# Attention and two expert layers on one core: TensorE's order written per unit, with the product with v one unit behind and 1/sum spread by two transposes

## The chip, the core and the metric

The kernel runs on one core of a Trainium2 chip. The metric is the device time of one execution, in microseconds (us); before the change the median of three runs is 1271.57 us (1271.40 to 1272.42). The engines are named as the profile names them: PE is TensorE (PEld its weight loads), DVE is VectorE, ACT is ScalarE, POOL is GpSimd, SP is SyncE, which only issues transfers here.

## What is computed

Attention with pooled queries, then a dense expert layer, then a second one. Inputs are float32, sizes are those of `setup`: 4 batches, 8 heads, 1152 positions, head width 64; d_model 512.

```python
q_pool = q.reshape(B, H, S // 2, 2, D).mean(axis=3)          # 576 queries a head
scores = scale * np.matmul(q_pool, k.transpose(0, 1, 3, 2))
scores = scores - np.max(scores, axis=-1, keepdims=True)
attn = np.exp(scores)
attn = attn / (np.sum(attn, axis=-1, keepdims=True) + 1e-09)
x = np.matmul(attn, v)                                       # -> (4 * 576, 512)

h = x @ w_in                                                 # 512 -> 2048
g = np.where(h >= 1, h, np.where(h <= -1, 0.0, (h + 1) ** 2 / 4))
x = g @ w_out                                                # 2048 -> 512

h = np.maximum(np.maximum(x @ w1, x @ w2), x @ w3)           # 512 -> 768
return h @ w_out2                                            # 768 -> 512
```

## The kernel before

**Units.** The attention is cut into 48 units: 4 batches b, in each 3 query blocks i of 192 pooled queries (`NB`), in each 4 pairs of heads p. Unit n is 12b + 4i + p; "unit 14" below is b = 1, i = 0, p = 2. A unit has 2 x 192 rows of scores against 1152 positions of k. They are worked on in three groups of 128 rows: group 0 and group 1 are the first 128 queries of the one head and of the other, group 2 is the rest, 64 rows of each. s0, s1 and s2 stand for the scores of the three groups (`qk`, L347: six matmuls, twelve for s2).

**One group.** `soft` makes the scores in PSUM, takes the row maximum on DVE (L361), the bias on ACT (L362) and the Exp on ACT (L363), which leaves float32 probabilities `pf` in SBUF and adds up their sum in `sm`. `turned` brings the probabilities into the transposed form `pt` that the product with v needs, and this goes two ways:

- In batches 1 to 3, groups 0 and 1 are split into a float16 high and low part `hl` (ACT L413, a subtraction on DVE L414) and transposed by a DMA, `pt<-hl` (L415), on SP's queue. Group 2 is transposed on TensorE, nine 128x128 pieces in float32 (L395), and split on the way out of PSUM (ACT L400, DVE L401).
- In batch 0 (`WHOLE`) all three groups are transposed on TensorE in float32 and copied out whole (L406, L408).

**1/sum.** `shares` forms 1/(sum + 1e-9) in `sm`, three columns of 128 rows, and spreads it into a tile of 128 x 192 that stands like the product with v: one row for each of the 2 x 64 columns of v, one column for each query. It does so by four float32 products with the identity (L376, L377), into the rest of the PSUM buffer that holds the nine transposed pieces. ACT copies it out as `R` (L379).

**The product with v.** `av` runs 54 matmuls in float16 (L432; 18 in float32 in batch 0, L427), and DVE multiplies the result by `R` (L445) into `xf`. After four units of a block `xh`, its float16 split, is ready for the dense layer.

**The dense layer** of a block is 8 tiles of up-projection (`ph`, L498, 24 matmuls each, followed by the gate on ACT, DVE and POOL, L503 to L509) and 4 of down-projection (`py`, L524, 48 matmuls each). `dense` hands them out in the turn up, up, down, in which each down belongs to the block before. The down-projections left over run after the last unit.

**Buffers in PSUM.** Scores and transposed tiles share two buffers of three banks (`place`, tag `sc`): they are given out in turn, so each `place` waits until the buffer of the one before last is read out. The product with v and the dense tiles share two banks (`psg`).

**The order.** TensorE runs in the order in which the program is written (`manual_schedule` for PE); the other engines are ordered by a scheduler that works from this text. The loop over slots, three for each unit, writes it: scores of the slot, in slot 0 the product with v of the unit two back, then `turned` of the slot before. `step` puts dense tiles in between, by a count of what is due (4 tiles for 3 slots, from slot 12 + `LAG` on). So from unit 8 on a unit has this row on TensorE: s0, product with v, a down, transposes of the unit before and 1/sum, s1, an up, s2, an up. The tables `K0`, `V0`, `K1`, `V1` name the slots in which the k and v of a batch are loaded, scaled and transposed; for batches 1 to 3 this is done in the last units of the batch before (L261 is the square that their scale comes from). The weights of the dense layer are converted during units 0 to 5, by `wgen` steps, `WR` a slot.

**After the last unit** the remaining downs run while the weights of the second layer are converted (from L150) into SBUF that the attention has given back; then the second layer, `p` (L737) and `po` (L754), takes the rest of the time.

Of the kernel before, what the change touches and what calls it, by code (L numbers as in the profile page):

```python
# [7 lines left out]
F32 = mybir.dt.float32  # L8
# [16 lines left out]
K1 = (-2, 0, 2)  # L25
V1 = (1, 3, 4)
WR = 1.5
OW = 130
OD0, T0 = -150, 48
LAG = 10  # L30
AVW = 0
POOL_KV = False
# [14 lines left out]
def body(ctx: ExitStack, tc: tile.TileContext, q, k, v, w_in, w_out, w1, w2, w3, w_o2, out):  # L47
# [320 lines left out]

    def shares(b, i, p, rs):

        sm = sums.pop((b, i, p))
        nc.vector.tensor_scalar(out=sm, in0=sm, scalar1=1e-9 * 2.0 ** 12, scalar2=None, op0=ALU.add)
        nc.vector.reciprocal(out=sm, in_=sm)
# [10 lines left out]
    def turned(b, i, p, who, pf):  # L384
# [4 lines left out]
        if who == 2 or WHOLE(b, p):  # L389

            tr = place(f"tr{key}")
            rs = tr[:, KT * P:KT * P + NB]
            tr = tr[:, :KT * P]
            for c in range(KT):
                nc.tensor.transpose(tr[:, c * P:(c + 1) * P], pf[:, c * P:(c + 1) * P], ident)  # L395
            copy = shares(b, i, p, rs) if who == 2 else None
            if not WHOLE(b, p):
                tr = tr.rearrange("p (c h q) -> p h c q", c=KT, h=2)
                hi, lo = pt[:, :, 0:KT, P:NB], pt[:, :, KT:2 * KT, P:NB]
                nc.scalar.activation(out=hi, in_=tr, func=AF.Copy)  # L400
                nc.vector.tensor_tensor(out=lo, in0=tr, in1=hi, op=ALU.subtract)  # L401
                copy()
                return
# [3 lines left out]
            else:  # L407
                nc.scalar.activation(out=pt[:, :, :, P:NB], in_=tr.rearrange("p (c h q) -> p h c q", c=KT, h=2),  # L408
                                     func=AF.Copy)
                copy()  # L410
            return
# [162 lines left out]
    def now(t):  # L574
        for gen in events.get(t, ()):
            next(gen)
# [5 lines left out]
    behind, todo = {}, []  # L582
    due = sent = wdue = 0.0
    slots = [(b, i, p, who) for b, i, p in units for who in range(3)]

    def step(t, share):

        nonlocal sent
# [5 lines left out]
    for t, (b, i, p, who) in enumerate(slots):  # L594
        n = t // 3
        if who == 0:
            exp_scale(b, i, p)
        behind[t] = soft(b, i, p, who)
        now(t)
        step(t, 0)  # L600
        if who == AVW and n >= 2:
            av(*todo.pop(0))
            step(t, .4)
        if t:
            turned(*behind.pop(t - 1))
        step(t, .8)
        if who == 2:
            todo.append((b, i, p))
        if who == 1 and n % 2 == 1 and n + 1 < len(units):
            q_prep(*units[n + 1])  # L610
        wdue += WR
        while wdue >= 1:
            with shift(OW):
                next(wgen, None)
            wdue -= 1
        step(t, 1.3)
    turned(*behind.pop(t))
    while todo:
        av(*todo.pop(0))
    order.__exit__(None, None, None)  # L620
# [217 lines left out]
```

## Time and profile before

| | |
|---|---|
| median of three runs | 1271.57 us |
| the profiled execution, its own time | 1269.06 us |
| its span, first to last instruction | 1267.2 us |
| PE busy | 1099.9 us, 87% |
| PEld busy | 892.9 us, 70% |
| DVE busy | 846.7 us, 67% |
| ACT busy | 687.3 us, 54% |
| POOL busy | 309.0 us, 24% |

The shares are means over the whole span. Units 0 to 13, the units in the middle of a batch, the units that also prepare the next batch, the rest after the last unit, and the second layer differ in what they hold, so each has its own shares. The start of a unit is read off the first matmul of its s0.

### The profile page before, as it was taken

What the parts mean: (1) busy time and instruction counts of PE and PEld (TensorE: products, weight loads), DVE (VectorE), ACT (ScalarE), POOL (GpSimd) and SP (SyncE); (2) the same over time, 40 slices, a digit from 0 to 9 for tenths busy, and PEclk for the clock granted to TensorE, in tenths of its full rate; (3) what the DMA queues carried; (4) which work ended last, traced back from release to release, by engine and by line L of the source; (5) the groups of instructions that cost most, each with busy time, mean ns of one, the idle gap of its engine ahead of it and who ended that gap; (6) DMA issues with size and microseconds to landing.
All of it is one profiled execution on the core that took longest, in us unless ns stands there. A gap on an engine that the chain in (4) does not pass through costs nothing. (4 is left out here: it accounts for less than half of the span.)

```text
span 1267.2 us, 27173 instructions
## 1 busy us (share of the span) xinstructions
PE 1099.9 (87%) x11346; PEld 892.9 (70%) x11346; DVE 846.7 (67%) x1406; ACT 687.3 (54%) x1193; POOL 309.0 (24%) x306
## 2 busy tenths in 40 slices
PE   0557799989999879899988999998968999999998
PEld 0334577767788768777776787787968877767774
DVE  4997776687777778777778977676997662232220
ACT  4777786666666666666656666665453421112111
POOL 1210113342223324222233422222654020000000
PEclk9989899999999899999988999999979999999999
DMA  9863313476555778555568655545422310000001
GB/s 314 247 179 123 92 27 72 113 155 119 107 107 99 135 164 175 101 103 104 102 146 177 123 95 95 95 82 136 160 100 83 117 52 31 9 18 26 18 17 42
DMA packets 273756, 134.94 MB, mean 106 GB/s; under 512 B 229089, under 2 KB 256737, under 8 KB 272609
## 3 DMA queue, kind: packets, MB, share of 16 engines
q1 hardware_dynamic: 273632, 133.20, 45.7%
q8 instruction: 89, 1.46, 0.5%
q14 instruction: 35, 0.28, 0.1%
HBM read 62.39 MB, written 9.44 MB: 57 GB/s over the span
## 5 line engine op out<-in xcount | busy, mean ns | idle before, releaser
L347 PE MATMUL sc<-kst,qst 128*64 128x512 f16 (+3 forms) x1152 | 179.1, 347 | 107.2 <-ACT pf L363 52.6
L361 DVE TENSOR_REDUCE st<-sc 128x1 f32<-128x1152 f32 x144 | 195.0, 1354 | 88.5 <-PE sc L347 88.4
L498 PE MATMUL ph<-xh,win 128*128 128x192 f16 x2304 | 219.8, 256 | 1.1 <-ACT t L503 0.6
L524 PE MATMUL py<-g,wou 128*128 128x192 f16 x2304 | 201.5, 247 | 15.0 <-POOL g L507 7.5
L737 PE MATMUL p<-yh,wm 128*128 128x288 f16 x1728 | 214.5, 286 | 0.0
L498 PEld LDWEIGHTS <-win 128*128 128x128 f16 x2304 | 203.0, 103 | 13.5 <-issue 8.3
L524 PEld LDWEIGHTS <-wou 128*128 128x128 f16 x2304 | 189.7, 98 | 22.6 <-issue 17.2
L347 PEld LDWEIGHTS <-qst 128*64 128x64 f16 (+1 forms) x1152 | 84.8, 108 | 170.5 <-issue 96.1
L737 PEld LDWEIGHTS <-wm 128*128 128x128 f16 x1728 | 169.0, 98 | 45.0 <-issue 0.4
L363 ACT ACTIVATE pf<-sc,st,esc 128x1152 f32<-128x1152 f32 x144 | 188.4, 1308 | 4.0
L505 POOL TENSOR_TENSOR rl<-t,rl 128x384 f32<-128x384 f32 x96 | 111.1, 1158 | 247.7 <-DVE rl L504 226.4
L362 ACT ACTIVATE st<-st,esc 128x1 f32<-128x1 f32 x144 | 42.1, 293 | 129.6 <-DVE st L361 129.2
L414 DVE TENSOR_TENSOR hl<-pf,hl 128x1152 f16<-128x1152 f32 x72 | 98.8, 1372 | 20.4 <-ACT hl L413 20.4
L395 PE MATMUL tr<-ident,pf 128*128 128x128 f32 x648 | 90.5, 288 | 20.8 <-ACT R L379 10.7
L507 POOL TENSOR_SCALAR g<-t,dgs 128x384 f16<-128x384 f32 x96 | 72.4, 754 | 134.2 <-DVE t L506 102.4
L395 PEld LDWEIGHTS tr<-ident,pf 128*128 128x128 f32 x648 | 76.1, 149 | 30.7 <-ACT R L379 14.4
L742 DVE TENSOR_TENSOR mx<-p,mx 128x288 f32<-128x288 f32 x48 | 21.9, 456 | 106.2 <-PE p L737 105.6
L745 ACT ACTIVATE h<-mx 128x288 f16<-128x288 f32 x48 | 21.2, 442 | 131.3 <-DVE mx L743 131.3
L432 PE MATMUL av<-pt,vhl 128*64 128x192 f16 x1944 | 87.1, 247 | 1.2 <-DMA pt<-hl 1.2
L432 PEld LDWEIGHTS <-vhl 128*64 128x64 f16 x1944 | 79.5, 110 | 10.3 <-issue 10.0
L413 ACT ACTIVATE hl<-pf 128x1152 f16<-128x1152 f32 x72 | 83.8, 1163 | 1.1
L509 DVE SCALAR_TENSOR_TENSOR g<-t,dgs,g 128x384 f16<-128x384 f32 x96 | 75.2, 783 | 12.1 <-POOL g L507 12.0
(167 smaller groups left out, 1338.4 us busy)
## 6 DMA issues: line engine op xcount, KB each, us to landing
kn<-in_k_dram SPq DMA_DIRECT2D x16, 576.0 KB, 4.6
vn<-in_v_dram SPq DMA_DIRECT2D x16, 576.0 KB, 4.4
raw_m<-in_moe_w_dram SPq DMA_DIRECT2D x12, 768.0 KB, 4.5
raw_in<-in_moe_w_in_dram SPq DMA_DIRECT2D x8, 1024.0 KB, 6.8
qn<-in_q_dram SPq DMA_DIRECT2D x24, 256.0 KB, 3.3
raw_ou<-in_moe_w_out_dram SPq DMA_DIRECT2D x10, 512.0 KB, 4.4
qst<-qst SPq DMA_DIRECT2D x48, 96.0 KB, 2.3
y_d<-ys SPq DMA_DIRECT2D x48, 96.0 KB, 2.0
```

The costliest lines, as they stand in the source:

```text
L347: nc.tensor.matmul(sc[m0:m1, n0:n1], qst[b, i, p][who][:, var, m0:m1], ks[:, h, n0:n1], start=(var == 0), stop=(var == 1))
L361: nc.vector.tensor_reduce(out=m, in_=sc, axis=AX.X, op=ALU.max, negate=True)
L363: nc.scalar.activation(out=pf, in_=sc, func=AF.Exp, bias=nb, scale=e, accum_out=sums[b, i, p][:, who:who + 1])
L395: nc.tensor.transpose(tr[:, c * P:(c + 1) * P], pf[:, c * P:(c + 1) * P], ident)
L413: nc.scalar.activation(out=hl[:, 0], in_=pf, func=AF.Copy)
L414: nc.vector.tensor_tensor(out=hl[:, 1], in0=pf, in1=hl[:, 0], op=ALU.subtract)
L432: nc.tensor.matmul(acc[64 * h:64 * h + 64], vhl[b, p][:, vi, h, c, :], pt[:, h, pi * KT + c, :], start=(c == 0 and e == 0), stop=(c == KT ...
L498: nc.tensor.matmul(ph[:, a], win[:, wi, kt, ff * P:(ff + 1) * P], x[:, xi, kt], start=(kt == 0 and e == 0), stop=(kt == KD - 1 and e == 2))
L505: nc.gpsimd.tensor_tensor(out=rl, in0=t2, in1=rl, op=ALU.add)
L509: nc.vector.scalar_tensor_tensor(out=g[:, 1, fs, :], in0=t2, scalar=gs, in1=g[:, 0, fs, :], op0=ALU.mult, op1=ALU.subtract)
L524: nc.tensor.matmul(py, wou[:, ff // 2, wi, ff % 2, m * P:(m + 1) * P], g[:, gi, ff, :], start=(ff == 0 and e == 0), stop=(ff == NF - 1 and ...
L737: nc.tensor.matmul(ph[:, :NB2], wm[:, wi, i, kt, ff * P:(ff + 1) * P], yh[:, yi, kt, n0:n0 + NB2], start=(kt == 0 and e == 0), stop=(kt == ...
```

## The change

TensorE's order is no longer counted out by `step` but written as a row of words for each unit, one row for batch 0 (`True`) and one for the others. "s" is a group's scores, "t" its `turned` ("t-" group 2 of the unit before), "r" `shares` of the unit before, "a1" the product with v of the unit one back, "d" the next dense tile, "q" the preparation of queries, "w" a step of the weights. Dense tiles begin with unit 6 (`DENSE`). `V1` prepares v one slot earlier in two of its steps. `shares` widens 1/sum on DVE to a tile `rb` of 128 x 192, transposes that in two pieces, and copies it out in two.

```diff
-V1 = (1, 3, 4)
+V1 = (1, 2, 3)
...
-LAG = 10
-AVW = 0
+ORDER = {True: "s0 t- d d r s1 t0 q s2 t1 a1 w d d w w",
+         False: "s0 t- d d r s1 t0 a1 s2 t1 q w d d w w"}
+DEPTH = 1
+DENSE = 6
...
-        for h in range(2):
-            rows = slice(64 * h, 64 * h + 64)
-            nc.tensor.matmul(rs[rows, 0:P], sm[:, h:h + 1].to_broadcast([P, 64]), ident, start=True, stop=True)
-            nc.tensor.matmul(rs[rows, P:NB], sm[:, 2:3].to_broadcast([P, 64]), ident[:, rows], start=True, stop=True)
-        R[b, i, p] = tp.tile([P, NB], F32, tag="R", bufs=3, name=f"R{b}_{i}_{p}")
-        return lambda: nc.scalar.activation(out=R[b, i, p], in_=rs, func=AF.Copy)
+        nc.vector.tensor_copy(out=rb, in_=sm.rearrange("p (a o) -> p a o", o=1).to_broadcast([P, 3, 64]))
+        r, half = R[b, i, p], slice(64, P)
+        nc.tensor.transpose(rs[:, 0:P], rb[:, 0:2].rearrange("p a o -> p (a o)"), ident)
+        nc.tensor.transpose(rs[:, P:2 * P], rb[:, 2, 0:1].to_broadcast([P, P]), ident)
+
+        nc.scalar.activation(out=r, in_=rs[:, :NB], func=AF.Copy)
+        nc.scalar.activation(out=r[half, P:NB], in_=rs[half, NB:2 * P], func=AF.Copy)
...
-            copy = shares(b, i, p, rs) if who == 2 else None
+            if who == 2:
+                R[b, i, p] = rs
...
-        d = (t - 12 - LAG) * 4 / 3 + share
-        while sent + 1 <= d:
-            next(dense, None)
-            sent += 1
...
-        if who == AVW and n >= 2:
-            av(*todo.pop(0))
-            step(t, .4)
...
+        elif kind == "r":
+            if n:
+                shares(*units[n - 1])
+        elif kind == "a":
+            if n >= int(num):
+                av(*units[n - int(num)])
+        elif kind == "d":
+            if n >= DENSE:
+                next(dense, None)
...
+    for n, (b, i, p) in enumerate(units):
+        for word in ORDER[WHOLE(b, p)].split():
+            attend(n, word)
```

The dense tiles still come in the turn up, up, down. A down takes two calls of `dense`, so the four "d" of a unit are two ups and one down: both ups stand ahead of "r", the down at the end.

What this moves is shown at three places of batch 2, in which unit 28 is block 1, pair 0. In the names the digits are block, pair and, for scores and transposed tiles, group (`tr_1_0_2` holds the transposes of group 2 of unit 28); the last number only tells buffers apart.

The first place is on PE, where unit 28's product with v starts. Before the change it follows s0 of unit 30 (`sc_1_2_0`):

```order
L347 LDWEIGHTS qst_1_2_6865
L347 MATMUL sc_1_2_0_6959<-kst_2_5086,qst_1_2_6865 128x512
L347 LDWEIGHTS qst_1_2_6865
L347 MATMUL sc_1_2_0_6959<-kst_2_5086,qst_1_2_6865 128x128
L432 LDWEIGHTS vhl_0_4806
L432 MATMUL av_1_0_6972<-pt_1_0_6591,vhl_0_4806 64x192
```

After it the product follows s1 of unit 29 (`sc_1_1_1`):

```order
L352 LDWEIGHTS qst_1_0_6633
L352 MATMUL sc_1_1_1_7049<-kst_1_5067,qst_1_0_6633 128x512
L352 LDWEIGHTS qst_1_0_6633
L352 MATMUL sc_1_1_1_7049<-kst_1_5067,qst_1_0_6633 128x128
L440 LDWEIGHTS vhl_0_4967
L440 MATMUL av_1_0_7066<-pt_1_0_6804,vhl_0_4967 64x192
```

The product with v has moved ahead by two groups of scores, the down-projection and one up, and it now stands between s1 and s2.

The second place is on PE too, where unit 28's 1/sum is spread, in unit 29. Before the change, between the last matmul of a down (`py`) and s1:

```order
L524 MATMUL py_1_1_6762<-g_1_5263,wou 128x192
L395 MATMUL tr_1_0_2_6815<-ident,pf_1_0_2_6643 128x128 x9
L376 MATMUL tr_1_0_2_6815<-ident,sm_1_0_6444 64x128
L377 MATMUL tr_1_0_2_6815<-ident,sm_1_0_6444 64x64
L376 MATMUL tr_1_0_2_6815<-ident,sm_1_0_6444 64x128
L377 MATMUL tr_1_0_2_6815<-ident,sm_1_0_6444 64x64
L347 LDWEIGHTS qst_1_0_6341
L347 MATMUL sc_1_1_1_6835<-kst_1_4810,qst_1_0_6341 128x512
```

After it, between the last matmul of the second up (`ph`) and s1:

```order
L506 LDWEIGHTS win
L506 MATMUL ph_2_7_7007<-xh_2_5804,win 128x192
L384 MATMUL tr_1_0_2_6962<-ident,rb_1_0_7042 128x128
L385 MATMUL tr_1_0_2_6962<-ident,rb_1_0_7042 128x128
L352 LDWEIGHTS qst_1_0_6633
L352 MATMUL sc_1_1_1_7049<-kst_1_5067,qst_1_0_6633 128x512
```

Two transposes stand in the place of four products, and the nine transposes of the same buffer have moved away from them, ahead of the two ups.

The third place is ACT, from the copy of unit 28's transposed tile (`pt_1_0<-tr_1_0_2`) in unit 29 on. Before the change:

```order
L400 ACTIVATE pt_1_0_6591<-tr_1_0_2_6815 128x2x9x64
L362 ACTIVATE st_1_1_1_6842<-st_1_1_1_6842,esc_1_1_6684 128x1
L363 ACTIVATE pf_1_1_1_6843,sm_1_1_6694<-sc_1_1_1_6835,st_1_1_1_6842,esc_1_1_6684 128x1152
L503 ACTIVATE t_1_2_4_6894<-ph_2_4_6869,hh_4156 128x384
L379 ACTIVATE R_1_0_6831<-tr_1_0_2_6815 128x192
L413 ACTIVATE hl_1_1_1_6920<-pf_1_1_1_6843 128x1152
L362 ACTIVATE st_1_1_2_6915<-st_1_1_2_6915,esc_1_1_6684 128x1
L363 ACTIVATE pf_1_1_2_6916,sm_1_1_6694<-sc_1_1_2_6902,st_1_1_2_6915,esc_1_1_6684 128x1152
```

After it:

```order
L410 ACTIVATE pt_1_0_6804<-tr_1_0_2_6962 128x2x9x64
L367 ACTIVATE st_1_1_0_6956<-st_1_1_0_6956,esc_1_1_6947 128x1
L368 ACTIVATE pf_1_1_0_6958,sm_1_1_6957<-sc_1_1_0_6949,st_1_1_0_6956,esc_1_1_6947 128x1152
L511 ACTIVATE t_1_2_6_6999<-ph_2_6_6974,hh_4001 128x384
L421 ACTIVATE hl_1_1_0_7062<-pf_1_1_0_6958 128x1152
L511 ACTIVATE t_1_2_7_7032<-ph_2_7_7007,hh_4001 128x384
L387 ACTIVATE R_1_0_7040<-tr_1_0_2_6962 128x192
L388 ACTIVATE R_1_0_7040<-tr_1_0_2_6962 64x64
L367 ACTIVATE st_1_1_1_7056<-st_1_1_1_7056,esc_1_1_6947 128x1
L368 ACTIVATE pf_1_1_1_7057,sm_1_1_6957<-sc_1_1_1_7049,st_1_1_1_7056,esc_1_1_6947 128x1152
```

The copy of 1/sum has become two (L387, L388), and they have moved from behind the Exp of s1 to ahead of it. The buffers move with the order: s2 (`sc_1_1_2`) was given the buffer of s1 before, and after the change that of the transposed tile, which the copies of 1/sum read last.

## Rows read from the trace of the kernel before

**Rows 1.** Windows by stage: start:end, length, busy (instructions) per engine, PEclk, DMA, GB/s.

```profile
148.86:163.03 14.17, 10.49 (x96) 7.50 (x96) 10.81 (x18) 11.47 (x18) 1.25 (x2) 1.00 0.07 15
163.03:177.55 14.52, 14.14 (x144) 11.27 (x144) 10.73 (x17) 13.91 (x22) 1.59 (x3) 1.00 0.20 42
...
206.82:284.61 77.79, 67.86 (x649) 56.02 (x648) 56.74 (x107) 47.76 (x83) 29.51 (x28) 0.91 0.59 130
284.61:399.45 114.84, 106.22 (x1339) 91.69 (x1338) 85.22 (x127) 75.47 (x136) 31.95 (x36) 1.00 0.57 107
399.45:516.24 116.79, 100.12 (x1166) 85.67 (x1164) 94.81 (x157) 73.05 (x130) 40.68 (x41) 0.93 0.72 148
...
614.67:710.60 95.93, 83.36 (x973) 71.61 (x972) 81.14 (x137) 61.40 (x111) 37.56 (x35) 0.93 0.72 150
...
858.25:979.97 121.72, 103.19 (x1235) 97.99 (x1233) 100.26 (x147) 55.20 (x88) 58.05 (x42) 0.93 0.42 123
```

**Rows 2.** Timeline, PE, one unit: start, busy, line, tiles, count [idle before <-releaser].

```profile
776.22 1.14 PE L347 MATMUL sc<-kst,qst 128*128 128x512 f16 x6
777.29 2.42 PE L432 MATMUL av<-pt,vhl 128*64 128x192 f16 x54
779.64 4.13 PE L524 MATMUL py<-g,wou 128*128 128x192 f16 x48
783.61 1.15 PE L395 MATMUL tr<-ident,pf 128*128 128x128 f32 x9
784.69 0.45 PE L376 MATMUL tr<-ident,sm 128*64 128x128 f32 x4
...
785.18 1.15 PE L347 MATMUL sc<-kst,qst 128*128 128x512 f16 x6
786.16 2.14 PE L498 MATMUL ph<-xh,win 128*128 128x192 f16 x24
789.54 1.17 PE L347 MATMUL sc<-kst,qst 128*64 128x512 f16 x12 [1.23 <-ACT pf L363]
790.64 2.15 PE L498 MATMUL ph<-xh,win 128*128 128x192 f16 x24
792.63 1.14 PE L347 MATMUL sc<-kst,qst 128*128 128x512 f16 x6
```

**Rows 3.** Timeline, DVE, the same unit.

```profile
786.37 1.36 DVE L361 TENSOR_REDUCE st<-sc 128x1 f32<-128x1152 f32 x1 [2.73 <-PE sc L347]
...
796.16 0.42 DVE L445 SCALAR_TENSOR_TENSOR xf<-av,Uv,R 128x192 f32<-128x192 f32 x1
```

**Rows 4.** Timeline, ACT, the same unit.

```profile
785.30 1.13 ACT L400 ACTIVATE pt<-tr 128x1152 f16<-128x1152 f32 x1 [0.67 <-PE tr L377]
...
788.09 1.31 ACT L363 ACTIVATE pf<-sc,st,esc 128x1152 f32<-128x1152 f32 x1
...
789.85 0.33 ACT L379 ACTIVATE R<-tr 128x192 f32<-128x192 f32 x1
```

**Rows 5.** DMA view of the transposing transfers of L415.

```profile
DMA to landing us min/median/max: 4.5/4.6/10.0
```

**Rows 6.** Windows, a unit that prepares the next batch.

```profile
479.60:496.90 17.30, 15.37 (x197) 13.29 (x194) 17.27 (x36) 10.71 (x21) 8.91 (x8) 1.00 0.84 175
```

**Rows 7.** Timeline, PE, another such unit.

```profile
454.49 2.00 PE L347 MATMUL sc<-kst,qst 128*64 128x512 f16 x12 [4.06 <-ACT R L379]
```

**Rows 8.** Timeline, PE, in the first batch.

```profile
144.82 1.17 PE L347 MATMUL sc<-kst,qst 128*64 128x512 f16 x12 [1.22 <-ACT pt L406]
146.44 1.20 PE L395 MATMUL tr<-ident,pf 128*128 128x128 f32 x9 [0.45 <-ACT pf L363]
...
216.53 2.18 PE L395 MATMUL tr<-ident,pf 128*128 128x128 f32 x9 [2.03 <-ACT R L379]
```

**Rows 9.** Timeline, ACT, after the last unit: the weights of the second layer.

```profile
885.51 2.59 ACT L150 ACTIVATE st_m<-raw_m 128x768 f32<-128x768 f32 x3 [4.93 <-DMA pt<-hl]
```

**Rows 10.** Timeline, DVE, after the last unit: the scaled operand of the second layer.

```profile
972.14 4.78 DVE L710 SCALAR_TENSOR_TENSOR yh<-yf,ysc,yh 128x576 f16<-128x576 f32 x4 [0.65 <-POOL yh L708]
```

More of the change, by code (lines that the diff above doesn't have):

```diff
@@ L367, in body, with shares @@
     R = {}
-    def shares(b, i, p, rs):
+    def shares(b, i, p):
         sm = sums.pop((b, i, p))
+        rs = R[b, i, p]
+        R[b, i, p] = tp.tile([P, NB], F32, tag="R", bufs=3, name=f"R{b}_{i}_{p}")
         nc.vector.tensor_scalar(out=sm, in0=sm, scalar1=1e-9 * 2.0 ** 12, scalar2=None, op0=ALU.add)
+        rb = tp.tile([P, 3, 64], F32, tag="rb", bufs=2, name=f"rb{b}_{i}_{p}")
         nc.vector.reciprocal(out=sm, in_=sm)
-        for h in range(2):
-            rows = slice(64 * h, 64 * h + 64)
-            nc.tensor.matmul(rs[rows, 0:P], sm[:, h:h + 1].to_broadcast([P, 64]), ident, start=True, stop=True)
-            nc.tensor.matmul(rs[rows, P:NB], sm[:, 2:3].to_broadcast([P, 64]), ident[:, rows], start=True, stop=True)
-        R[b, i, p] = tp.tile([P, NB], F32, tag="R", bufs=3, name=f"R{b}_{i}_{p}")
-        return lambda: nc.scalar.activation(out=R[b, i, p], in_=rs, func=AF.Copy)
+        nc.vector.tensor_copy(out=rb, in_=sm.rearrange("p (a o) -> p a o", o=1).to_broadcast([P, 3, 64]))
[4 more added lines that the diff above has]
+        nc.scalar.activation(out=r[half, P:NB], in_=rs[half, NB:2 * P], func=AF.Copy)
     def whole(pt):
@@ L391, in turned @@
             tr = place(f"tr{key}")
-            rs = tr[:, KT * P:KT * P + NB]
+            rs = tr[:, KT * P:KT * P + 2 * P]
             tr = tr[:, :KT * P]
@@ L401, in turned @@
                 nc.vector.tensor_tensor(out=lo, in0=tr, in1=hi, op=ALU.subtract)
-                copy()
                 return
@@ L409, in turned @@
                                      func=AF.Copy)
-                copy()
             return
@@ L582, in body @@
     behind, todo = {}, []
[L583 to L588, printed above, removed]
-        d = (t - 12 - LAG) * 4 / 3 + share
-        while sent + 1 <= d:
-            next(dense, None)
-            sent += 1
[L594 to L600, printed above, removed]
-        if who == AVW and n >= 2:
-            av(*todo.pop(0))
-            step(t, .4)
[L604 to L616, printed above, removed]
@@ L617, in body, with attend @@
-    turned(*behind.pop(t))
-    while todo:
-        av(*todo.pop(0))
+    wdue = 0.0
+    def attend(n, word):
+        nonlocal wdue
+        b, i, p = units[n]
+        kind, num = word[0], word[1:]
+        if kind == "s":
+            who = int(num)
+            if who == 0:
+                exp_scale(b, i, p)
+            behind[n, who] = soft(b, i, p, who)
+            now(3 * n + who)
+        elif kind == "t":
+            key = (n - 1, 2) if num == "-" else (n, int(num))
+            if key in behind:
+                turned(*behind.pop(key))
+        elif kind == "r":
[7 more added lines that the diff above has]
+                next(dense, None)
+        elif kind == "q":
+            if n % 2 == 1 and n + 1 < len(units):
+                q_prep(*units[n + 1])
+        elif kind == "w":
+            wdue += WR
+            while wdue >= 1:
+                with shift(OW):
+                    next(wgen, None)
+                wdue -= 1
@@ L620, in body @@
+    for n, (b, i, p) in enumerate(units):
+        for word in ORDER[WHOLE(b, p)].split():
+            attend(n, word)
+    last = len(units)
+    turned(*behind.pop((last - 1, 2)))
+    shares(*units[last - 1])
+    for n in range(last - DEPTH, last):
+        av(*units[n])
     order.__exit__(None, None, None)
```

## The prediction

> **What bounds the kernel now.** I read the stages first, as windows cut at the starts of units [rows 1]. From 858 us on the program is another matter (its tail is below, its last part is TensorE at full pace), so the change is worth something before that, in 48 units of attention. In the stretch from 284.61 to 399.45 seven units take 114.84 us, 16.41 each, and TensorE is busy 106.22: it waits 8.62, which is 1.23 a unit, though it is the engine that is fullest.
>
> The timeline of TensorE in one such unit shows where [rows 2]: from 776.22 to 792.63 its pieces follow each other without a break, but for one wait of 1.23 us ahead of the scores of the row rest (s2). The releaser is the Exp of the scores just before (s1): s2 was given the PSUM buffer of s1, and only one up-projection tile stands between them. The reader should see the chain behind s1 in the two engine timelines: the maximum takes 1.36 us on DVE [rows 3], the bias and the Exp end at 789.40 on ACT [rows 4], and s2 starts at 789.54; from s1's end at about 786.2 that is 3.3 us, and the cover is 2.1. A wait that nothing else of TensorE's fills, and that every unit of a stage repeats in which TensorE is the fullest engine, is worth its whole length.
>
> **The change, part by part.** All sums are against the profiled execution, 1269.06 us; the median of the runs shown is 2.5 us above it, which I add at the end.
>
> *Steady units (numbers 14 to 20, 27 to 32, 38 to 46: 22 of them).* From starts to next starts in rows 2: s0 1.07, product with v 2.35, down 3.97, nine transposes 1.08, spreading 1/sum 0.49, s1 0.98, s2 1.10, a tile of up 1.98 (790.64 to 792.63). The new order has s0, transposes, up, up, spread, s1, product with v, s2, down. Spreading becomes two transposes; at 1.08 for nine they are 0.24 together, so 0.25 is saved. The sum is 1.07 + 1.08 + 3.96 + 0.24 + 0.98 + 2.35 + 1.10 + 3.97 = 14.75, if nothing waits. What is late next is checked one by one, with 3.3 us as the price of a reduction and Exp. Exp of s0 ahead of s1: cover 5.28 (transposes, two ups, spread) against 3.3 plus 1.13 for the copy of the transposed tile on ACT [rows 4]: 0.8 to spare. Exp of s1 ahead of the next s0: cover 7.4; the reduction now stands behind a subtraction (L414) of as many elements as its own 1.36 [rows 3] and two short gate operations on DVE, so about 5.6: free. Exp of s2 ahead of its transposes: cover 5.04 (down and s0), chain 3.3 plus about 0.9 of queued DVE work: 0.8 to spare, the tightest. The evictions of 1/sum ahead of s2 (they share its buffer): two of at most 0.33 each [rows 4], done about 1.3 us after the spread, cover 3.3. So I take 14.8: 22 x 1.6 = -35. The ends are 14.75 (-37) and 15.5, with both spare times of 0.8 eaten by a DVE that runs late (-20).
>
> The new copy that widens 1/sum on DVE has no row. It is 128x192 float32, so it lies near the 0.42 of the other 128x192 operation [rows 3]; between 0 and 0.6. DVE is busy 85.22 of 114.84 us there [rows 1], 12.2 a unit; with the copy 12.6 of 14.8, so it has room. The new second eviction adds under 0.33 to an ACT that is busy 75.47 of 114.84.
>
> The product with v one unit behind adds a wait: it needs the transposing transfers of its own unit's s1, which had a unit more. Laid out in the new unit, the subtraction of s1 ends about 15 us after the unit's start; the transfer lands 4.6 us after its issue [rows 5], at 19.7; the product starts at 14.8 + 7.3 = 22.1. It is hidden with 2.4 us to spare. Behind it on TensorE stand s2 and down.
>
> *Units that also prepare the next batch's k and v (21 to 26, 33 to 37: 11 units, 116.79 + 95.93 = 212.7 us in rows 1).* Here TensorE waits up to 4.06 us for the eviction of 1/sum [rows 7], which stands in ACT's queue behind the square of a new k tile (L261), and the granted clock of both stretches is 0.93 against 1.00 in the steady one [rows 1]. After the change that eviction has 3.3 us of cover instead of 2.1, and s1 has 5.3. What remains is DVE: busy 94.81 + 81.14 = 176 us, 16.0 a unit, 16.4 with the copy. That DVE can run that full shows in the unit at 479.60, with 17.27 of 17.30 [rows 6]. I take 17.7: 11 x 17.7 = 194.7, -18. The ends are 16.4 (-32) and only the spread saved (-3).
>
> *The first batch (units 0 to 13), whose products are whole float32.* Two things count against the change. The dense work starts 1.33 units earlier, so two ups (3.96) and two downs (7.94) move in here: +11.9. And with both ups ahead of s1, only one transposed tile stands between s1 and s2, so s2 waits for its copy, 1.22 us, and the next transposes for an Exp, 0.45; a unit without dense work shows both waits [rows 8]. Units 7 to 9 wait 0.4 each (14.52 - 14.14 in the first, rows 1), so six units lose 1.3 each: +8. Against that: the spread 14 x 0.25 = -3.5, waits in units 6 and 10 to 13 (14.17 - 10.49 and 77.79 - 67.86, 13.6 us in all, rows 1; one of 2.03 in rows 8), of which the moved work fills about half, -6.5, and in units 0 to 5, where weights are converted, s1 loses the product with v as cover, +2. Sum +12; ends +5 and +25.
>
> *The tail (858.25 to 979.97, from unit 47's start to the second block, rows 1).* 11.9 us of dense work have left it, but TensorE is not alone in it: the second block's weights can only be converted when the attention's buffers are free, which ACT begins at 885.51, 27.3 us after the unit's start, behind the last transposing transfer [rows 9]. The chain from there runs through ACT, DVE and GpSimd to the scaled operand of the second block, whose first quarter is written 1.2 us after 972.14 [rows 10], 88 us on; the second block starts at 979.97 only because TensorE has downs left until then. The subtraction of unit 47 comes some 2 us sooner in the new unit, so the chain would end at 25 + 88 = 113 instead of 121.7: -9. TensorE's own work alone would give 11.9 and the unit's 1.2 (16.0 to 14.8): -13, the lower end; the upper is 0, with a later chain.
>
> Sum: -35 - 18 + 12 - 9 = -50; 1269.06 - 50 = 1219, plus 2.5: **1221 us**.
>
> **One rule against it.** The nine transposes take 1.08 us where the granted clock is 1.00 [rows 1, 2], 0.12 each. The Trainium skill says otherwise in "TensorE: Matmul & The Clock Gate", Part 4 (PE-mode transpose): a transpose costs some 275 ns in a kernel, and transposes do not raise the clock. By that figure two would be 0.55, dearer than the 0.49 they replace, and the estimate would be 1236; the trace disagrees in the steady units.
>
> **The rivals.** (a) Transposes at the lower clock level. After a wait nine took 2.18 [rows 8], 0.24 each; two would cost 0.48, what they replace: 48 x 0.25 = +12, 1233 us. Against it: they stand behind two ups without a break. The rule above belongs here. (b) DVE and the weight chain keep their pace: the units with preparation give 3 instead of 18 and the tail nothing, 1221 + 15 + 9 = 1245. For it: both stretches have DVE at 0.8 and more of the time [rows 1]; against: the wait in them is one for ACT. (c) **Slower**: the transfers land late, and the product with v waits for them in each unit of batches 1 to 3. From the layout above a unit then takes 15.05 + landing - 7.33; it loses to 16.41 from a landing of 8.7 us on. The median is 4.6, the longest 10.0 [rows 5]; at 10.0 it is 17.7, 36 x 1.3 = +47, and the first batch's +12: about 1330. Against it: the long ones are few. (d) The new order does not do what it says: s2 is again given a buffer that the Exp of s1 frees. The cover would be the product with v alone, 2.35 against 2.1 now; only 0.25 and the spread's 0.25 are won in each steady unit, the first batch costs 12, and the whole comes out at 1271.57 - 11 + 12 = 1272, the same. The built program speaks against it: s2 there waits for the eviction of 1/sum. (e) DVE fills up in the units with preparation and TensorE ends the tail: 1221 - 14 - 4 = 1203.
>
> **How the numbers follow.** Forecast 0.64, (a) 0.08, (b) 0.15, (e) 0.05, (c) 0.05, (d) 0.03. The range goes from 1203, case (e), to 1246, just past (b); it leaves out (c) and (d), half of (e) and some of the spread about (b). About 0.2%, 2.5 us, is what this kernel's measurement can tell from no change. Faster 0.92, same 0.03, slower 0.05.
>
> **What would show it.** Right: unit starts 14.8 us apart with no wait in the steady stretches, the wait of the scores for Exp gone there, two transposes of 0.12 for 1/sum, the second block starting some 50 us earlier, at about 930. Wrong: a wait of the product with v for its transfer (c), of s2 for Exp (d), periods of 19 and more with preparation (b), a granted clock below 1.00 in steady units (a), or a first batch longer by much more than 12 us.

## The result and the profile after

The changed kernel takes 1240.3 us in the median of four runs (1239.76 to 1242.11), against 1271.49 before: 0.976 of it, 95% interval 0.9743 to 0.9777. The forecast was 1221, with a range of 1203 to 1246. The sign and the range hold; of the 50 us that were forecast 31 came. The profiled execution has a span of 1237.9 us, 29.3 less than before.

The stages of the changed kernel, as windows cut at the starts of units (columns as in [rows 1]): units 0 to 5, 6 to 13, 14 to 20, 21 to 26, 27 to 32, 33 to 37, 38 to 46, and from unit 47 to the second layer.

```profile
27.53:164.50 136.97, 83.36 (x517) 56.58 (x518) 109.76 (x192) 98.74 (x154) 20.94 (x15) 0.78 0.55 159
164.50:312.93 148.43, 130.71 (x1287) 107.92 (x1286) 99.17 (x184) 96.28 (x164) 46.76 (x49) 0.94 0.39 78
312.93:421.45 108.52, 102.68 (x1297) 89.82 (x1296) 92.29 (x138) 76.62 (x144) 31.65 (x39) 1.00 0.65 115
421.45:526.78 105.33, 92.89 (x1129) 81.05 (x1127) 92.45 (x165) 74.51 (x137) 42.07 (x39) 0.98 0.82 164
526.78:618.58 91.80, 87.69 (x1113) 77.01 (x1111) 77.07 (x113) 63.81 (x121) 25.86 (x32) 1.00 0.62 111
618.58:706.61 88.03, 78.09 (x944) 68.06 (x942) 76.73 (x141) 61.65 (x114) 37.48 (x34) 0.98 0.83 162
706.61:840.28 133.67, 130.90 (x1668) 115.52 (x1666) 113.16 (x166) 96.96 (x179) 32.73 (x42) 1.00 0.58 101
840.28:948.08 107.80, 86.94 (x1023) 82.55 (x1021) 89.95 (x136) 54.75 (x91) 44.63 (x33) 0.94 0.44 130
```

Set beside the same stages of before (most of them in [rows 1]; the others by the same unit starts):

| stage | before, us | after, us | change | forecast |
|---|---|---|---|---|
| units 0 to 5 | 121.7 | 137.0 | +15.3 | about +0.5 |
| units 6 to 13 | 135.8 | 148.4 | +12.7 | about +11.5 |
| steady units, 22 | 360.9 | 334.0 | -26.9 | -35 |
| units with preparation, 11 | 212.7 | 193.4 | -19.4 | -18 |
| unit 47 to the second layer | 121.7 | 107.8 | -13.9 | -9 |
| second layer and start | | | +2.8 | 0 |

Two places lack the gain: units 0 to 5, and the steady units. A clean steady unit looks as it was laid out. The timeline of PE in unit 29:

```profile
557.82 1.14 PE L352 MATMUL sc<-kst,qst 128*128 128x512 f16 x6
558.79 1.15 PE L404 MATMUL tr<-ident,pf 128*128 128x128 f32 x9
559.78 4.12 PE L506 MATMUL ph<-xh,win 128*128 128x192 f16 x48
563.74 0.27 PE L384 MATMUL tr<-ident,rb 128*128 128x128 f32 x1
563.85 0.27 PE L385 MATMUL tr<-ident,rb 128*128 128x128 f32 x1
563.96 1.14 PE L352 MATMUL sc<-kst,qst 128*128 128x512 f16 x6
565.02 2.42 PE L440 MATMUL av<-pt,vhl 128*64 128x192 f16 x54
567.28 1.14 PE L352 MATMUL sc<-kst,qst 128*64 128x512 f16 x12
568.35 4.13 PE L532 MATMUL py<-g,wou 128*128 128x192 f16 x48
...
572.32 1.14 PE L352 MATMUL sc<-kst,qst 128*128 128x512 f16 x6
574.79 1.20 PE L404 MATMUL tr<-ident,pf 128*128 128x128 f32 x9 [1.33 <-ACT pf L368]
```

From 557.82 to 572.32 nothing waits: 14.50 us, 0.25 under the sum of the prediction. But the last row shows the next unit, 30, with a wait of 1.33 us ahead of its transposes, for the Exp of s2 of unit 29. The unit starts show the pattern: of units 14 to 20 and 27 to 32 the odd ones take 14.5, the even ones 15.3 to 18.1; unit 38 takes 17.6, and units 39 to 46 take 14.5 to 14.6, odd and even. Three windows, units 28 to 30:

```profile
541.29:557.82 16.53, 14.73 (x189) 12.84 (x187) 14.15 (x20) 11.86 (x22) 4.05 (x5) 1.00 0.69 92
557.82:572.32 14.50, 14.50 (x187) 12.83 (x186) 11.80 (x20) 9.59 (x20) 4.62 (x6) 1.00 0.64 130
572.32:588.37 16.05, 14.72 (x187) 12.83 (x186) 14.20 (x20) 11.84 (x22) 3.21 (x5) 1.00 0.58 94
```

Why the Exp of s2 is late in unit 29 stands in two other timelines. First GpSimd:

```profile
567.98 0.99 POOL L321 TENSOR_TENSOR qn<-qn 128x384 f32<-128x384 f32 x1 [3.31 <-DMA qn<-in_q_dram]
568.95 0.58 POOL L515 TENSOR_SCALAR g<-t,dgs 128x384 f16<-128x384 f32 x1
569.50 0.99 POOL L513 TENSOR_TENSOR rl<-t,rl 128x384 f32<-128x384 f32 x1
```

and then DVE:

```profile
569.57 1.35 DVE L517 SCALAR_TENSOR_TENSOR g<-t,dgs,g 128x384 f16<-128x384 f32 x1 [1.68 <-POOL g L515]
570.84 0.41 DVE L453 SCALAR_TENSOR_TENSOR xf<-av,Uv,R 128x192 f32<-128x192 f32 x1
571.16 0.54 DVE L514 SCALAR_TENSOR_TENSOR t<-t,rl 128x384 f32<-128x384 f32 x1
571.63 1.35 DVE L366 TENSOR_REDUCE st<-sc 128x1 f32<-128x1152 f32 x1
```

These rows are read from the bottom. The reduction of s2 starts at 571.63, though s2 ended at about 568.4. Ahead of it on DVE stands the gate's last step (L517), which waits 1.68 us for GpSimd's step before (L515). That step had its operand, but stood in GpSimd's queue behind the sum of two query rows (L321), and this waited 3.31 us for a load of queries that a later unit needs. So a transfer that nobody needs yet holds the Exp that TensorE needs next. In unit 30, where GpSimd waits for no load, the reduction of s2 starts 0.8 us after s2's end (584.47 to 585.27), and not 3.2. The last sum of query rows in this kernel runs in unit 38 (710.49); behind it no load of queries is left, and there the even units take 14.5 like the odd ones. The kernel before has the same wait on GpSimd, in unit 29:

```profile
560.07 0.99 POOL L316 TENSOR_TENSOR qn<-qn 128x384 f32<-128x384 f32 x1 [4.00 <-DMA qn<-in_q_dram]
```

There it cost TensorE nothing that shows: the units of that stretch all take 16.4.

Of the time above 14.5 in the steady stretches, 8.1 us lie in units 16, 18, 20, 28, 30 and 32. Another 6.6 us lie in units 14 and 38, each the third of its batch: there TensorE waits for the Exp of s2 (1.20 and 1.69) and, ahead of the product with v, for a transposing transfer (1.57 and 1.08).

The waits of PE over the whole program (total, times, longest):

```profile
PE tr L404 <- ACT pf L368: 17.4, 18, 2.3
PE sc L352 <- ACT pt L415: 17.2, 11, 3.1
PE sc L352 <- ACT pf L368: 15.1, 9, 4.6
PE tr L384 <- ACT pt L417: 11.5, 5, 4.2
PE sum_in L195 <- ACT wou L180: 10.1, 2, 7.9
...
PE av L440 <- DMA pt<-hl: 2.7, 2, 1.6
```

Before the change the wait of the scores for Exp stood first among PE's:

```profile
PE sc L347 <- ACT pf L363: 52.6, 34, 4.0
```

It has fallen from 52.6 us to 15.1, and none of it is left in the steady units. In its place stand the transposes that wait for an Exp (17.4), and, in the first batch, copies (17.2 and 11.5). In unit 1 the sums over `w_in`, which TensorE has in its queue ahead of unit 2, wait long for weights (10.1 us, where it was 5.2 before):

```profile
76.74 0.83 PE L195 MATMUL sum_in<-wou,ones 128*32 128x512 bf16 x12
79.71 0.39 PE L195 MATMUL sum_in<-wou,ones 128*32 128x512 bf16 x2 [2.14 <-ACT wou L180]
88.02 0.61 PE L195 MATMUL sum_in<-wou,ones 128*32 128x512 bf16 x2 [7.92 <-ACT wou L180]
```

### The profile page after: what moved, and what is told of

Read it like the earlier page. It is cut to its first block, busy times and chain, and to the rows that moved or that the text cites. A ratio compares the mean times of both kernels' runs of the same rounds, so it can differ in the third digit from the quotient of the medians.

```text
span 1237.9 us, 26735 instructions
## 1 busy us (share of the span) xinstructions
PE 1077.9 (87%) x11058; PEld 881.2 (71%) x11058; DVE 857.5 (69%) x1454; ACT 696.8 (56%) x1241; POOL 302.9 (24%) x306
## 4 chain that ended last, share of the span: by engine, by line
PE 41%; DVE 17%; issue 7%; DMA 7%; ACT 6%; POOL 4%; SPq 2%; ACTq 0%; POOLq 0%; DVEq 0%
PE p L752 17%; PE po L769 5%; PE ph L506 5%; PE py L532 4%; DVE st L366 4%; DMA qn<-in_q_dram 3%; PE sc L352 3%; PE tr L404 3%; PE av L440 2%; DVE g L517 2%; DVE hl L422 2%; DVE t L514 2%; ACT pf L368 1%; POOL g L515 1%; ACT hl L421 1%
## 5 line engine op out<-in xcount | busy, mean ns | idle before, releaser
L532 PE MATMUL py<-g,wou 128*128 128x192 f16 x2304 | 201.1, 248 | 22.4 <-POOL g L515 7.8
L506 PE MATMUL ph<-xh,win 128*128 128x192 f16 x2304 | 203.2, 249 | 4.9 <-ACT py L536 2.6
L366 DVE TENSOR_REDUCE st<-sc 128x1 f32<-128x1152 f32 x144 | 194.1, 1348 | 18.0 <-PE sc L352 17.8
L506 PEld LDWEIGHTS <-win 128*128 128x128 f16 x2304 | 195.1, 99 | 7.5 <-issue 5.7
L513 POOL TENSOR_TENSOR rl<-t,rl 128x384 f32<-128x384 f32 x96 | 103.7, 1083 | 185.3 <-DVE rl L512 185.3
L404 PE MATMUL tr<-ident,pf 128*128 128x128 f32 x648 | 98.9, 306 | 26.3 <-ACT pf L368 17.4
L422 DVE TENSOR_TENSOR hl<-pf,hl 128x1152 f16<-128x1152 f32 x72 | 104.3, 1449 | 22.7 <-ACT hl L421 22.6
L404 PEld LDWEIGHTS tr<-ident,pf 128*128 128x128 f32 x648 | 83.5, 161 | 40.9 <-ACT pf L368 24.8
L515 POOL TENSOR_SCALAR g<-t,dgs 128x384 f16<-128x384 f32 x96 | 70.7, 738 | 97.0 <-DVE t L514 91.4
L517 DVE SCALAR_TENSOR_TENSOR g<-t,dgs,g 128x384 f16<-128x384 f32 x96 | 74.2, 781 | 16.4 <-POOL g L515 16.2
```

What stands on the lines that cost most here:

```text
L366: nc.vector.tensor_reduce(out=m, in_=sc, axis=AX.X, op=ALU.max, negate=True)
L422: nc.vector.tensor_tensor(out=hl[:, 1], in0=pf, in1=hl[:, 0], op=ALU.subtract)
L506: nc.tensor.matmul(ph[:, a], win[:, wi, kt, ff * P:(ff + 1) * P], x[:, xi, kt], start=(kt == 0 and e == 0), stop=(kt == KD - 1 and e == 2))
L513: nc.gpsimd.tensor_tensor(out=rl, in0=t2, in1=rl, op=ALU.add)
L517: nc.vector.scalar_tensor_tensor(out=g[:, 1, fs, :], in0=t2, scalar=gs, in1=g[:, 0, fs, :], op0=ALU.mult, op1=ALU.subtract)
L532: nc.tensor.matmul(py, wou[:, ff // 2, wi, ff % 2, m * P:(m + 1) * P], g[:, gi, ff, :], start=(ff == 0 and e == 0), stop=(ff == NF - 1 and ...
```

## The experiments

The kernel before took 1266 to 1268 us in the later runs, not 1271, so kernels are compared by their ratio to the runs of before made beside them. Spans and stages below are of one profiled execution each. The changed kernel was run again:

> The changed kernel again, unaltered, to stand beside the other kernels on one chip. 0.976 of the kernel before, 0.974 to 0.978.

Measured: 1233.17 us, 0.9733 (0.9701 to 0.9765), a little under what was expected; span 1232.8. Its stages agree with those above but for some 5 us in the first batch, which is as far as two executions of one kernel lie apart there.

| kernel | us | ratio to before (95%) | span | units 0 to 5 | units 6 to 13 | units 14 to 46 | 47 to second layer |
|---|---|---|---|---|---|---|---|
| after_again | 1233.2 | 0.9733 (0.9701 to 0.9765) | 1232.8 | 136.2 | 144.4 | 526.7 | 108.0 |
| q_sum | 1220.5 | 0.9643 (0.9614 to 0.9672) | 1217.8 | 139.6 | 136.0 | 519.1 | 107.8 |
| w_spread | 1226.9 | 0.9700 (0.9664 to 0.9736) | 1223.5 | 125.9 | 147.0 | 525.3 | 108.4 |
| a2_first | 1232.7 | 0.9739 (0.9709 to 0.9768) | 1231.9 | 132.9 | 145.8 | 526.8 | 110.6 |
| early_old | 1223.2 | 0.9658 (0.9628 to 0.9687) | 1221.4 | 126.9 | 145.9 | 525.6 | 106.8 |
| order_only | 1231.8 | 0.9732 (0.9700 to 0.9765) | 1231.2 | 130.8 | 144.9 | 529.8 | 107.2 |
| spread_only | 1272.8 | 1.0048 (1.0033 to 1.0063) | 1271.2 | 122.6 | 138.8 | 574.8 | 120.8 |
| dense8 | 1241.0 | 0.9798 (0.9764 to 0.9831) | 1240.3 | 136.2 | 137.0 | 527.4 | 125.8 |
| best1 | 1221.7 | 0.9642 (0.9602 to 0.9682) | 1222.1 | 135.0 | 137.9 | 524.0 | 109.2 |
| best2 | 1219.6 | 0.9626 (0.9600 to 0.9653) | 1217.3 | 131.5 | 136.4 | 523.0 | 107.9 |
| best3 | 1216.9 | 0.9601 (0.9557 to 0.9646) | 1214.1 | 126.8 | 142.4 | 518.6 | 109.5 |
| best3_prod | 1221.9 | 0.9659 (0.9632 to 0.9687) | 1217.5 | 123.8 | 140.7 | 525.2 | 110.3 |

Stages are those of each profiled execution, in us, cut at the starts of units.

**The even steady units: the query load on GpSimd.** The sum of query rows gets a tile of its own with one buffer. It must then follow the split into float16 (L245, L246) of the pair before, by which time its load has long landed.

```diff
-        qp = qn[:, :, 0, :]
+        qp = qp_.tile([P, 6, D], F32, tag="qa", bufs=1, name=f"qa{key}")
         nc.gpsimd.tensor_tensor(out=qp, in0=qn[:, :, 0, :], in1=qn[:, :, 1, :], op=ALU.add)
```

> The changed kernel, but the sum of two query rows is written to a tile of its own with one buffer, so that GpSimd's add (L321) can't be due before the split of the pair before has been done, when its load has long landed. Theory (GpSimd's queue stands still for the query load, and behind it the gate, DVE's L517 and the reduction of s2): the seven even units of the steady stretches fall from 15.3 to 18.1 us to 14.5, together 113.3 - 101.5 = -12, the units with preparation give up to 3 more: 1225 to 1229 us. Rival (DVE's own queue is too full, the load has nothing to do with it): even units stay where they are, 1239 to 1241.

Measured: 1220.54 us, 0.9643 against the 0.9733 of after_again, which is 11 us; the spans of the two profiled executions differ by 15.0. Units 27 to 32 as a window:

```profile
513.16:600.68 87.52, 87.25 (x1113) 77.00 (x1111) 75.16 (x113) 63.68 (x121) 27.08 (x32) 1.00 0.63 117
```

87.52 us is six times 14.59, and PE is busy 87.25 of it. GpSimd's two rows in unit 29 of this kernel show that L321 now waits for DVE, and not for a load:

```profile
545.64 0.58 POOL L245 TENSOR_SCALAR qpre<-qa,sqq 128x384 f16<-128x384 f32 x1 [5.30 <-ACT st L367]
547.47 1.00 POOL L321 TENSOR_TENSOR qa<-qn 128x384 f32<-128x384 f32 x1 [1.24 <-DVE qpre L246]
```

That the load on GpSimd's queue made the even units from 16 to 20 and from 28 to 32 late is shown, and DVE's fullness alone as the cause is out for them: with the same work on DVE the waits are gone, but for 0.3 in units 18 and 30. The edit has a second effect that goes the same way and was not separated: the split now reads the new tile, so the loaded tile is free sooner and the load is issued earlier. Counted through, the load at 517.33 is for the sum at 575.17; in the changed kernel the load at 563.05 is for the sum at 567.98. Units 14 to 46 gave 7.6 us, less than the 12 to 15 expected, since units 14, 26 and 38, each the third of a new batch, still wait 2.5 to 3.5; for these three DVE's own queue is not excluded. Some 5 came in the first batch, which had not been expected.

**The first units: three kernels.** In the changed kernel three things differ in units 0 to 5: the product with v stands behind the second transposes, 1/sum behind the copy of the transposed tile, and the three weight words in the last third of the unit. Each kernel here adds a row for units 0 to 5.

```diff
+EARLY = "s0 t- a2 d d r s1 t0 q s2 t1 w d d w w"      # a2_first
+EARLY = "s0 t- w d d r s1 t0 q w s2 t1 a1 w d d"      # w_spread
+EARLY = "s0 a2 t- w d d s1 t0 q w s2 t1 w d d"        # early_old; 1/sum inside t-, ahead of its copy
...
-        for word in ORDER[WHOLE(b, p)].split():
+        for word in (EARLY if n < 6 else ORDER[WHOLE(b, p)]).split():
```

> The changed kernel, but in units 0 to 5 the product with v stands two units behind, right after the transposes and ahead of 1/sum (unit 5 also does the one left over at its end). Theory (in the first units, without dense work, the product with v was the cover for the copy of the transposed tile, on which 1/sum waits, and for the Exp of s0, on which s1 waits): units 0 to 5 fall from 137 to about 124 us, 1227. Rival (the loss comes from the weight steps, which now stand together at the unit's end): unit 1 stays at 38 us, only 1 to 1.5 us in each of units 2 to 5 comes back, 1235.

> The changed kernel, but in units 0 to 5 the three words for the weights stand one behind each group again (after the transposes, after the query word, after the second transposes), as they did before, in place of all behind the product with v. Theory (weight steps come too late, so that the sums over w_in, L195, which TensorE has in its queue ahead of unit 2, wait for them): unit 1 falls from 38 to about 28 us, 1230. Rival (the product with v is the missing cover): 0 to -3, 1237 to 1240.

> The changed kernel, but in units 0 to 5 the row of the kernel before: product with v two units behind and right after s0, 1/sum spread right behind the transposes and ahead of their copy, weight words behind each group. The spread stays the two transposes. Theory (the loss of the first units is the order there, weights and covers together): units 0 to 5 take 121 to 124 us as before, where the changed kernel takes 136 to 137; 14 us less in all, 0.962 of before. Rival (the chip is bound there by the conversion of weights on DVE and ACT, whatever the order): no more than the 10 that the weight words alone gave, 0.966.

Measured: a2_first 1232.67 us (0.9739), no different from the changed kernel; its unit 1 stays at 38.1, its units 2 to 5 give 3.2 together. w_spread 1226.86 (0.9700); unit 1 falls from 38.2 to 27.7, and the sums over `w_in` run without a wait. PE at the end of its unit 1 (L196 is the sums there; the last row is cut off by the window):

```profile
74.34 4.01 PE L436 MATMUL av<-pt,vn 128*64 128x192 f32 x36
78.28 1.25 PE L196 MATMUL sum_in<-wou,ones 128*32 128x512 bf16 x16
79.47 0.60 PE L353 MATMUL sc<-kst,qst 128*128 128x512 f16 x2
```

early_old, the whole old row, measured 1223.16 us, 0.9658, and takes 126.9 us for units 0 to 5, hardly other than w_spread's 125.9. Unit 1 takes 38.0 to 38.3 us in all six traces with the weight words at the unit's end, and 25.8 to 29.7 in all six in which they are spread. So the place of the weight words is the cause, by some 10 us of this stage; in the whole time w_spread's interval overlaps that of after_again, and early_old's does not. The product with v as cover and the place of 1/sum add nothing that these runs can tell. Of the 15 us some 5 stay even under the old row. best3_prod below has that row with the four products and takes 123.8 there, so about 3 of the 5 go with the spread by transposes; the rest is open.

**The tail and the dense start.**

```diff
-DENSE = 6
+DENSE = 8
```

> The changed kernel with the dense tiles begun in unit 8 in place of 6: four ups and two downs, 15.9 us of TensorE's work, go from units 6 to 13 to the tail. If the tail is bound by TensorE as its work is written, the tail grows by 15.9 and the first batch shrinks by up to as much: within 3 us of the changed kernel. Rival (the tail is bound by the chain through the second layer's weights, and TensorE has room there): the tail grows by less than 8, and the kernel is 8 to 12 us faster, 0.967 of before.

Measured: 1241.0 us, 0.9798. The tail as a window:

```profile
827.13:952.97 125.84, 105.40 (x1216) 100.82 (x1214) 102.04 (x148) 56.91 (x97) 63.26 (x43) 0.93 0.41 122
```

It grows by 17.8 us for 15.9 us of moved work, and units 6 to 13 shrink by 7.4. The whole is 8 us slower than after_again, beyond the 3 us of the expectation. So the tail's end goes with the work written there, and an earlier dense start is a gain: the first batch does half of it in time in which TensorE waits.

**What each part of the change gave.** Here the old spread is put into the new order, and the new spread into the old order.

```diff
-        nc.tensor.transpose(rs[:, 0:P], rb[:, 0:2].rearrange("p a o -> p (a o)"), ident)
-        nc.tensor.transpose(rs[:, P:2 * P], rb[:, 2, 0:1].to_broadcast([P, P]), ident)
+        for h in range(2):
+            rows = slice(64 * h, 64 * h + 64)
+            nc.tensor.matmul(rs[rows, 0:P], sm[:, h:h + 1].to_broadcast([P, 64]), ident, start=True, stop=True)
+            nc.tensor.matmul(rs[rows, P:NB], sm[:, 2:3].to_broadcast([P, 64]), ident[:, rows], start=True, stop=True)
```

> The changed kernel, but 1/sum is spread by the four float32 products as before, from the three columns, and copied out in one. By rows of the kernel before the two transposes save 0.25 us in each of 48 units: if none of it is hidden, 1252. Rival (it is hidden in the units in which TensorE waits anyway, the first 14 and the units with preparation): it counts in some 22 units, 1246. Second rival (the copy that widens 1/sum and the second copy on ACT cost more than the transposes save): 1237 to 1240.

> The kernel before with one part of the change alone: 1/sum is widened on DVE, spread by two transposes and copied out in two; the order stays counted out by slots, the product with v two units behind. Theory (the transposes save 0.25 us of TensorE's time wherever it doesn't wait, and in the old order the second copy on ACT and the wider tile lie under the wait of s2): some 22 to 40 units give 0.25, 5 to 10 us less than before. Rival (1/sum now waits for DVE's copy, which TensorE has in its queue right behind the transposes of the same unit, ahead of s1): each unit loses about 0.4, +10 to +20.

Measured: order_only 1231.83 us, 0.9732, the same as the changed kernel's 0.9733; spread_only 1272.83 us, 1.0048 (1.0033 to 1.0063), a little slower than before. So the order carried the gain, and the spread by transposes nothing that shows in the whole. In a unit without a wait the spread does count: 14.89 us in order_only, 14.50 in the changed kernel. PE of order_only in unit 40 (L383 and L384 are the products there):

```profile
734.52 0.45 PE L383 MATMUL tr<-ident,sm 128*64 128x128 f32 x4
734.79 0.29 PE L384 MATMUL tr<-ident,sm 128*64 128x64 f32 x4
735.01 1.15 PE L352 MATMUL sc<-kst,qst 128*128 128x512 f16 x6
```

From the first product, 734.52, to s1 it is 0.49 us; in unit 29 of the changed kernel, 563.74 to 563.96, 0.22. The even units' waits took it up, and in the first batch order_only was 5 us better. In spread_only the steady units gain too, 112.2 for units 14 to 20 against 114.84, but the units with preparation lose 9.3 us: 121.5 and 100.6 against 116.79 and 95.93 in [rows 1]. The wait of the scores for Exp in units 21 to 37 is, before and in spread_only:

```profile
PE sc L347 <- ACT pf L363: 23.8, 13, 4.0
```

```profile
PE sc L347 <- ACT pf L363: 43.0, 17, 6.5
```

There the widening copy and the second eviction come on top of full queues on DVE and ACT; that it is these two was not tested apart.

**Repairs together.** best1 has q_sum and w_spread; best2 also puts an up back between s1 and s2 in the rest of the first batch; best3 has the row of early_old, that up, and the query tile from unit 6 on; best3_prod is best3 with the four products.

```diff
-ORDER = {True: "s0 t- d d r s1 t0 q s2 t1 a1 w d d w w",
+ORDER = {True: "s0 t- d r s1 t0 q d s2 t1 a1 w d d w w",      # best2, best3, best3_prod
```

> The changed kernel with two repairs together: the sum of query rows in a tile of its own, and the weight words behind each group in units 0 to 5. Alone they gave 20 and 14 us of span in the runs so far. Theory (they lie in different stages, so they add up): 30 to 34 less than the changed kernel beside it, 0.95 of before. Rival (the first units are bound by DVE's conversion of weights, so the gain there shrinks when the queries come in another order): 20 to 24 less.

> The same two repairs, and in the first batch the second up goes back between s1 and s2 (before: up, up, 1/sum, s1, transposes, s2). Theory (s2 there waits 1.22 for the copy of the only tile that stands between, and the next transposes 0.45 for an Exp; an up of 1.98 covers both): six units with dense work lose these waits, 7 to 10 less than with the two repairs alone. Rival (s1, with only one up ahead of it, now waits for the Exp of s0 instead): no less, within 3 us.

> The order of early_old in units 0 to 5, an up between s1 and s2 in the rest of the first batch, and from unit 6 on the sum of query rows in a tile of its own. Theory (three losses in three stages, each by its own mechanism, so they add up: 14, 7 and 12 us): 33 less than the changed kernel, 0.950 of before. Rival (as when two repairs were put together, the first units lose again what the weight words give, for a reason not yet seen): 0.960.

> The kernel of best3 (three repairs) with the four float32 products in place of the two transposes, as order_only is to the changed kernel. There units without a wait took 14.89 us in place of 14.51, but the whole was no slower, since waits elsewhere took it up. Theory (with the waits of the even units gone, 0.38 counts in each of the 20 or so units that don't wait, and part of the others): 8 to 13 us slower than best3, 0.967 to 0.971 of before. Rival (the products are worth as much as the transposes, because they need no widening copy on DVE and no second copy on ACT where those engines are late, in the first batch and in the units with preparation): within 3 us of best3, 0.958 to 0.963.

Measured: best1 0.9642, no better than q_sum alone, so the two don't add up: its units 0 to 5 take 135.0, where w_spread took 125.9. One step of it shows in unit 3, where PE's spread of 1/sum waits 3.87 us. Here is that row, with one of DVE and one of ACT:

```profile
109.82 0.33 PE L385 MATMUL tr<-ident,rb 128*128 128x128 f32 x1 [3.87 <-DVE sqq L97]
107.94 0.33 DVE L383 COPY rb<-sm 128x192 f32<-128x192 f32 x1
108.67 1.10 ACT L418 ACTIVATE pt<-tr 128x1152 f32<-128x1152 f32 x1
```

The releaser that the row names is not the likely one: the transposes don't read `sqq`, and their operand `rb` was written by 108.27. What ended just before them is ACT's copy of the transposed tile (L418, done at 109.77), for which the same step waits in the changed kernel (11.5 us in five waits). Why the two repairs don't add up is thus open. best3, which leaves the first queries as they were, has 126.8 there again. It has the lowest median of the study: 1216.87 us, 0.9601 (0.9557 to 0.9646), span 18.7 under the changed kernel; but its interval overlaps those of q_sum, best1 and best2, so these runs don't show it to be faster than q_sum alone. Of the 33 us that its theory added up, 16 came; its units 6 to 13 keep 142.4, where q_sum has 136.0. Which of the edits takes that back is open. best2 is 0.9626, within the interval of best1; its units 6 to 9 fall from 64.5 to 60.9 and 10 to 13 rise by 2. best3_prod is 0.9659: 0.0058 above best3, with intervals that touch. Its units without a wait take 14.89 again, 14 to 46 together 525.2 against 518.6, and the first batch is 4.7 us shorter. So in these two traces the transposes give 6.6 us in units 14 to 46 and lose part of it in the first batch. Units 14 and 38 go the other way: with the products they take 16.2 to 17.1 us (best3_prod and order_only), and 17.5 or more in every kernel with the new order and the transposes.

## Why the prediction was right in sign and 19 us too low

**The bound was read rightly.** The wait of s2 for the Exp of s1, repeated in each steady unit, was worth its length: with both ups ahead and another buffer for s2 it is gone, and a unit without other waits takes 14.50 where 14.75 was summed. The rows behind it ([rows 2 to 4]) hold: nine transposes 0.99, 1/sum 0.22, two ups 3.96, s1 1.06, product 2.26, s2 1.07, down 3.97. DVE's widening copy takes 0.35, between the ends that were given.

**Steady units: the cover that was named as the tightest failed.** The Exp of s2 ahead of its transposes was given 0.8 us to spare, "3.3 plus about 0.9 of queued DVE work". The 0.9 was the mis-sized term: from the end of s2 at about 568.4 to the start of its reduction at 571.63 it is 3.2 in unit 29. For DVE's own work it was right, 0.8 in unit 30. What made it 3.2 was not on DVE's list of work but on GpSimd's queue, a sum that waits for a load; the prediction never looked at that queue, though the wait stands in the trace of before (4.00 us in unit 29). -27 came instead of -35, between the ends that were given (-37 and -20). q_sum takes this cause away, and units 27 to 32 then take 87.5: 14.6 each. The rest of the loss lies in units 14 and 38, which the prediction counted among the units without preparation; q_sum leaves them at 17.6 and 18.7. A part goes with the spread by transposes, without which they are 1 to 2 us shorter; the rest of their cause was not tested.

**The first batch: +28 instead of +12, beyond the upper end of +25.** The step that failed is "s1 loses the product with v as cover, +2": with the spread's saving it gave units 0 to 5 about +0.5, and they came out at +15.3. It took the wrong part of the move: the words for the weights were moved too, from behind each group to the unit's last third, and their cost was not worked out at all. Spreading them again takes 10 us off (w_spread). About 3 more go with the spread of 1/sum, which was taken as a saving here too (best3 against best3_prod), and some 2 are open. The rest of the first batch, +12.7 (+8.7 in after_again), agrees with dense tiles moved in, s2 waiting 1.22 for its copy and the waits that they fill.

**Units with preparation: -19.4 against -18.** 17.6 a unit, as taken (17.7). But the reason was only half the one given. TensorE's waits fell by 6.9 us (from 29.2 to 22.4, length less busy in [rows 1] and in the windows above); its busy time fell by 12.5, of which the spread can be about 3. The granted clock rose from 0.93 to 0.98 there, which the prediction named and put no price on. DVE, which it took for the limit, is busy 15.4 of the 17.6 us. The change also prepares v a slot earlier (`V1`), and no run tests that apart.

**The tail: -13.9 against -9,** just beyond the lower end, which TensorE's own work gave (-13). dense8 shows why: the tail follows the work written in it. The chain through the second layer's weights is near then: its first products wait 2.7 and 1.0 us for ACT and DVE, and the second layer takes 2.4 longer.

**The spread.** 0.25 a unit was taken, and 0.27 to 0.38 is what a clean unit shows. But the whole kernel doesn't show it, and on the old order it is a loss: rows of one stage were used for all 48 units, though in the first batch and beside preparation it gains nothing or loses. That the extra copies on DVE and ACT are the reason there is likely, but not shown.

**The rivals.** (a) The transposes ran at the higher clock in steady units (granted clock 1.00; 0.11 from start to start). (b) The units with preparation became 19.4 us shorter, so they did not keep their pace. (c) The product with v waits for its transfer twice in the program, 2.7 us; the spare time was shorter than laid out, since the subtraction of s1 ends 16.1 us after the start of unit 30, not 15. (d) s2 has its new buffer. (e) DVE didn't fill up, and the sum stayed above 1221. That 1240 lies within the range is in part luck: its upper end was made for (b), and what cost the 19 us, GpSimd's queue and the words for the weights, stands in no rival.

## What to carry to other kernels

When work is moved, list for each moved word every queue that it has instructions on, and ask of each in-order queue what waits there for a transfer; a cover of 0.8 us is worth nothing as long as that is not done. An instruction that waits for a load early, though its result is needed late, belongs behind something that comes late: a buffer of its own with one slot did that here, for 11 us. Cut the program into stages before an edit is priced, and price it in each: the spread by transposes gains in one and loses in another.

## What the runs showed of the hardware

GpSimd can hold DVE up. L517 on DVE takes 0.60 us where GpSimd is idle, as in this row of unit 30 of the changed kernel:

```profile
572.89 0.60 DVE L517 SCALAR_TENSOR_TENSOR g<-t,dgs,g 128x384 f16<-128x384 f32 x1
```

At 569.57 in unit 29, beside GpSimd's L513 from 569.50 to 570.49, it takes 1.35: it ends some 0.4 after GpSimd does, as if it had run only then. That is 0.75 us more on the chain to the Exp of s2. The Trainium skill says in "SBUF — State Buffer" (SBUF: two separate sides) that a DVE instruction with two inputs in SBUF and a GpSimd instruction that reads SBUF share a pair of ports, which the one that starts first holds for its whole length while the other is blocked. This row agrees: L517 reads two tiles of SBUF and starts 0.07 us after L513.

The two transposes of 1/sum have records of 0.27 us each in unit 29, at granted clock 1.00, but start 0.11 apart (563.74, 563.85, then s1 at 563.96). So it is the distance of starts that goes into a sum, as the prediction took it.
